# A retention layer and a gMLP block on one core: all five instruction queues in a new order, more warm-up matmuls, and a semaphore that one more kind of job may raise

## The chip, the core and the metric

The kernel runs on one core of a Trainium2 chip. TensorE (PE) multiplies matrices; its weight loads are listed apart as PEld. VectorE (DVE), ScalarE (ACT) and GpSimd (POOL) do elementwise work. SyncE (SP) issues the DMAs, which 16 DMA engines carry out. Each engine works through its own queue strictly in the order in which the program was written, and engines wait for each other by semaphores. TensorE writes its results to PSUM, which is split into banks; ACT and DVE read them from there. The metric is the device time of one execution in microseconds (us).

## The reference, cut to what matters

```python
B, H, S, D = 8, 8, 576, 64
scores = scale * np.matmul(q, k.transpose(0, 1, 3, 2))
ret = scores * Dmat[None]            # Dmat[h, s, t] = gamma[h] ** (s - t) for s >= t, else 0
x = np.matmul(ret, v)                # heads side by side: (8, 576, 512)
h = gelu(x @ w_in)                   # 512 -> 1024, tanh form
u, v = h[..., :512], h[..., 512:]
v_n = (v - mean) / np.sqrt(var + 1e-6) * g_ln
v_s = np.einsum('ts,bsd->btd', w_sg, v_n) + b_sg[None, :, None]
out = x + (u * v_s) @ w_out
```

## The kernel before, in words

Because `Dmat` is a product of powers, the attention is computed in blocks with a running state. The eight sequences go in four pairs `p`; a pair has nine row tiles of 128 rows, in five blocks (line 158). Block 0 of a pair holds one tile (64 rows of each sequence); blocks 1 to 4 hold two tiles each. So there are 20 blocks `b` (0, 5, 10 and 15 are the small ones) and 36 tiles `i`.

For each block, SP loads q, k and v (`a_load`, lines 338 to 351: 512 KB each, 1024 KB for the q of two blocks together, 2 x 128 KB in a small block). `a_prep` (line 364) casts them to bf16 and multiplies q and v by powers of gamma, on POOL except in block 0, where DVE takes q and ACT takes k. TensorE transposes q and k (`a_T`, line 431) and DVE brings them out of PSUM (`a_Tev`, line 450). TensorE forms the scores (`a_S`, line 492, one or two halves `g` a block), and DVE masks them (`a_Sev`, lines 505 and 508). `a_Z` (line 532) forms the state terms k'v, which DVE adds to the running state (`a_Zsum`) and ACT rounds (`a_Zev`). `a_O` (line 568) adds up the attention output of a block: 16 or 32 small matmuls for the block itself and 8 for the state terms whose rows of the array go with the bank they write. The other 8, the swapped state terms, come in a job of their own, `a_O2` (line 614): another part of the array adds into a place that `a_O` has just written, so they may start only when `a_O`'s matmuls have ended. ACT brings the output out of PSUM as bf16 (`a_Oev`, line 636), and this is the input `x` of the block that follows.

For each tile, `m_V` (line 647) makes the v half (4 matmuls with 512 columns), ACT applies gelu (line 654), DVE takes mean and variance (lines 662, 663), POOL makes the factors (`m_rs`, lines 667 to 670) and ACT normalises (`m_norm`, lines 679 and 682). `m_U` (line 697) makes the u half, with gelu on ACT (line 707). When five tiles of a sequence are ready, eight jobs `m_W` (line 715) multiply by `w_sg`, and DVE multiplies with u (`m_Wg`, line 725). `m_O` (line 745) multiplies by `w_out`; x is added, and `m_store` writes the tile out.

How `a_O2` waits is decided when the program is written (lines 396 to 416 and 614 to 619). `a_O` of any block but a pair's first sets `pend[b] = None`. The next job on TensorE that calls `mark` lets one of its first matmuls raise the semaphore `swap`; since matmuls end in order, that tells that `a_O` has ended, and `a_O2` waits for the count. If no such job comes between, `a_O2` begins with `nc.tensor.drain()`: TensorE starts nothing until all its matmuls have ended. Before the change, jobs of `a_T`, `a_S`, `a_Z`, `m_V`, `m_U`, `m_W` and `m_O` call `mark`; `a_O` does not, nor does `build_wT`. A matmul that raises `swap` does not carry the usual semaphore of its job, so the reader of the job's result is tied to its last matmul (`fence`, `unfence`).

Weights: the halves of `w_in` come as 1024 KB each (`win_load`, line 256: half 1 is for V, half 0 for U), and DVE and ACT cast one part each (lines 273 and 275). `w_sg` is loaded in three parts, cast (line 304), and transposed by `build_wT`; `w_out` follows.

The order of all queues is a list, `ORDER` (line 20): job numbers in the order in which the program is written, so each engine's own queue is the list cut down to that engine. An entry `f1`, `f2` or `f4` is a filler (lines 234 to 240): a matmul of zeros in f32 of 128, 256 or 512 columns, which the profile shows as two instructions, on a PSUM bank that nobody reads. Fillers stand among TensorE's jobs before the first tiles. PSUM has two buffers `pp` (transposes, scores, attention outputs) and four buffers `d` (all else, fillers too); of the load buffers `ld` there are eight. `Planner.run` (line 91) gives each new tile the buffer whose last user stands earliest in the list, so a new order also changes who waits for whose buffer.

Of the kernel before, what the change touches and what calls it, by code (L numbers as in the profile page):

```python
# [14 lines left out]
Act = mybir.ActivationFunctionType  # L15
# [2 lines left out]
PR = dict(PB0=10000.0, O=4000.0, PB=9900.0, S=2000.0, S2=400.0, Z=1901.0, V=6000.0, V2=900.0, U=1260.0, W=4000.0, WS=19000.0, slack=60.0, pen=500.0)  # L18

ORDER = (  # L20
# [33 lines left out]
)  # L54


# [56 lines left out]
def kernel(  # L113
# [12 lines left out]
    nc = tc.nc  # L126
# [199 lines left out]
    cur = {}  # L326
# [71 lines left out]
    def mark(ins, what):  # L398
        waiting = [b for b, on in pend.items() if on is None]
        if waiting:  # L400
            cur["swap"] = cur.get("swap", 0) + 1
            ins.then_inc(swap, 1)
            tc.no_tile_sem_insts.add(ins.ins.name)
            fenced[what] = f"swap{cur['swap']}"
            tc.add_to_no_dep_group(fenced[what], ins.ins)
            for b in waiting:
                pend[b] = cur["swap"]

    def fence(ins, what):
        if what in fenced:  # L410
            tc.declare_fence(ins.ins, group=fenced[what])
# [156 lines left out]
    def a_O(b):  # L568
        ns, zs = RB[b % NBK][0], st.pop((b, "zs"))
        cs = 64 * ns  # L570
        ot = psP.tile([128, 2, 512], F32, name="pp", tag=bank("pp"))
        st[b, "ot"] = ot
        begun = set()

        def mm(bank, kk, hh, lhsT, rhs):
            c = kk % 2
            j = 2 * hh + kk // 2
            nc.tensor.matmul(ot[64 * c:64 * c + 64, bank, j * cs:(j + 1) * cs], lhsT, rhs,  # L578
                             start=(bank, c) not in begun, stop=True, skip_group_check=True)
            begun.add((bank, c))  # L580

        def ap(hh, bank):
            zb = zs[bank]
# [22 lines left out]
        for n in range(max(len(P[0]), len(P[1]))):  # L606
            for l in P:
                if n < len(l):
                    l[n]()
        if b % NBK:  # L610
            st[b, "O2"] = (ap(0, 1), ap(1, 0))
            pend[b] = None
# [13 lines left out]
    def a_Oev(b, c, eng="ACT"):  # L626
        p, n = divmod(b, NBK)
        ns, m, _ = RB[n]
        cs = 64 * ns
        if n == 0 and c == 0:  # L630
            xTs[p] = new("xT", [128, NT, KK, 128], BF)
        tile_, col = (m + c, 0) if ns == 2 else (m, cs * c)
        s_ = ns if joint(b) else 4
        dst = xTs[p][:, tile_, :, col:col + cs].rearrange("p j (i s) -> p j i s", s=s_)
        src = st[b, "ot"][:, c, :KK * cs].rearrange("p (j s i) -> p j i s", j=KK, s=s_)
        nc.scalar.activation(dst, src, Act.Copy)  # L636


    vgs, mvs, vns = {}, {}, {}
# [498 lines left out]
```

## Time and profile before

| what | value |
| --- | --- |
| time of a run, median of three | 207.34 us (207.1 to 207.71) |
| the profiled execution's own time | 208.13 us |
| its span in the profile | 206.4 us |
| mean granted TensorE clock in it | 0.965 |
| TensorE matmuls busy | 190.6 us, 92% of the span |
| weight loads, DVE, ACT, POOL busy | 129.5, 144.6, 117.3, 118.4 us |

How to read it: the span runs from the first to the last instruction of the profiled execution, and 1.7 us of its own time lie outside. An engine's busy time is the sum of its instructions without overlaps. The two lines of digits over the span that matter here are PE, the busy share of each slice of 5.16 us in tenths, and PEclk, the clock that TensorE was granted, in tenths of full speed. In lists, a group has its line of the kernel, the engine, the operation, the tile that it writes `<-` what it reads, the shapes and the count. In the chain of waits, each piece has its start, its length, and the engine with the line that ended last; `SPq` is SP issuing a DMA.

### The profile page before, as it was taken

How to read it: one execution, taken by the hardware profiler on the slowest of the kernel's cores; microseconds unless marked ns; L12 is line 12 of the kernel's file. 1: busy time of each engine (PE TensorE's matmuls, PEld its weight loads, DVE VectorE, ACT ScalarE, POOL GpSimd, SP SyncE). 2: the span in 40 equal slices, each digit the busy share in tenths (PEclk: the TensorE clock that was granted, in tenths of full speed). 3: DMA queues.
4: the chain of work that ended last, by engine and by line, in shares of the span. 5: the costliest groups of instructions: out<-in, count | busy, mean ns of one | idle time of the engine just before them, and what ended most of it. 6: DMA issues, size and time to landing. Idle time of an engine off the chain costs nothing.

```text
span 206.4 us, 7490 instructions
## 1 busy us (share of the span) xinstructions
PE 190.6 (92%) x3183; PEld 129.5 (63%) x3212; DVE 144.6 (70%) x281; ACT 117.3 (57%) x210; POOL 118.4 (57%) x167
## 2 busy tenths in 40 slices
PE   5946899999999999999999999999999999999991
PEld 3525647667757767567675675676576585566760
DVE  4268559886795768836982788477977788476672
ACT  5045739796787745777547636756535765335300
POOL 8594299969839999516993575960594260022000
PEclk9995579999999999999999999999999999999999
DMA  6999999999999848969999999999979983939455
GB/s 154 258 340 330 388 350 242 267 357 375 300 263 342 273 123 121 260 146 352 274 235 196 303 242 258 238 258 292 328 177 218 169 244 107 204 91 215 139 144 205
DMA packets 93908, 50.45 MB, mean 244 GB/s; under 512 B 45034, under 2 KB 87282, under 8 KB 93874
## 3 DMA queue, kind: packets, MB, share of 16 engines
q1 hardware_dynamic: 93856, 49.96, 93.0%
q8 instruction: 25, 0.41, 0.8%
q14 instruction: 9, 0.07, 0.1%
q10 hardware_dynamic: 18, 0.00, 0.0%
HBM read 32.79 MB, written 9.44 MB: 205 GB/s over the span
## 4 chain that ended last, share of the span: by engine, by line
PE 84%; DMA 10%; issue 2%; ACT 1%; SPq 1%; DVE 0%
PE wp L715 20%; PE hu L697 16%; PE hv L647 15%; PE op L745 15%; PE pp L578 7%; DMA uT<-in_moe_w_in_dram 5%; PE pp L492 4%; PE pp L431 3%; PE zp L532 2%; DMA ld<-in_moe_w_sg_dram 2%; DMA ld<-in_k_dram 2%; PE op L740 1%; PE wtp L839 1%; SPq L351 1%; ACT xT L636 1%
## 5 line engine op out<-in xcount | busy, mean ns | idle before, releaser
L505 DVE TENSOR_TENSOR ret<-pp,msk 128x1024 bf16<-128x1024 f32 x32 | 38.6, 1216 | 8.0 <-PE pp L492 7.9
L715 PE MATMUL wp<-wT,vn 128*128 128x288 bf16 x256 | 40.8, 286 | 0.0
L654 ACT ACTIVATE vg<-hv 128x512 f32<-128x512 f32 x36 | 21.2, 595 | 28.0 <-PE hv L647 17.7
L647 PE MATMUL hv<-w_in,xT 128*128 128x512 bf16 x128 | 35.8, 388 | 1.4 <-issue 0.3
L394 POOL TENSOR_TENSOR vb<-ld,gpow 128x1024 bf16<-128x1024 f32 (+1 forms) x20 | 34.4, 1730 | 4.3 <-DVE uT L725 4.0
L725 DVE TENSOR_TENSOR uT<-wp,uT 128x288 bf16<-128x288 f32 x64 | 27.6, 450 | 12.8 <-PE wp L715 10.4
L697 PE MATMUL hu<-xT,w_in 128*128 128x256 bf16 (+1 forms) x320 | 35.7, 262 | 0.1
L745 PE MATMUL op<-w_out,uT 128*128 128x512 bf16 (+1 forms) x135 | 33.9, 373 | 0.6
L667 POOL TENSOR_SCALAR mv<-mv 128x2 f32<-128x2 f32 (+1 forms) x20 | 4.5, 224 | 50.8 <-DVE mv L663 50.1
L697 PEld LDWEIGHTS <-w_in 128*128 128x128 bf16 x320 | 27.9, 98 | 5.5 <-issue 0.3
L715 PEld LDWEIGHTS <-vn 128*128 128x128 bf16 x256 | 25.1, 98 | 8.0
L394 POOL TENSOR_TENSOR qb<-ldq,gpow 128x1024 bf16<-128x1024 f32 x14 | 26.5, 1901 | 5.3 <-DMA ldq<-in_q_dram 5.3
L662 DVE BATCH_NORM_STATS2 bst<-vg 128x6 f32<-128x512 f32 x36 | 24.6, 682 | 6.9 <-ACT vg L654 6.7
L636 ACT ACTIVATE xT<-pp 128x512 bf16<-128x512 f32 (+1 forms) x40 | 20.9, 549 | 14.2 <-PE pp L578 14.2
L682 ACT ACTIVATE vn<-vg,mv 128x512 bf16<-128x512 f32 x32 | 25.5, 808 | 4.0 <-POOL mv L670 3.8
L707 ACT ACTIVATE uT<-hu 128x512 bf16<-128x512 f32 x36 | 21.0, 593 | 10.8 <-PE hu L697 10.8
L765 DVE TENSOR_TENSOR ob<-op,xr 128x512 f32<-128x512 f32 (+1 forms) x28 | 18.3, 667 | 8.7 <-PE op L745 5.2
L647 PEld LDWEIGHTS <-xT 128*128 128x128 bf16 x144 | 13.8, 100 | 13.6 <-issue 1.4
L745 PEld LDWEIGHTS <-uT 128*128 128x128 bf16 x148 | 13.8, 98 | 11.9
L715 PE MATMUL wp<-wT,vmid 128*128 128x288 bf16 x64 | 18.4, 288 | 0.0
L668 POOL TENSOR_TENSOR mv<-mv,mhalf 128x2 f32<-128x2 f32 (+1 forms) x20 | 13.7, 685 | 1.7
L384 POOL CAST kb<-ld 128x1024 bf16<-128x1024 f32 x14 | 14.3, 1038 | 0.0
(104 smaller groups left out, 234.2 us busy)
## 6 DMA issues: line engine op xcount, KB each, us to landing
ld<-in_k_dram SPq DMA_DIRECT2D x16, 512.0 KB, 8.1
ld<-in_v_dram SPq DMA_DIRECT2D x16, 512.0 KB, 6.3
out_dram<-ob SPq DMA_DIRECT2D x31, 256.0 KB, 3.6
ldq<-in_q_dram SPq DMA_DIRECT2D x7, 1024.0 KB, 8.7
out_dram<-ob SPq DMA_DIRECT2D x10, 128.0 KB, 3.5
xT<-in_moe_w_sg_dram SPq DMA_DIRECT2D x2, 576.0 KB, 8.3
ld<-in_k_dram SPq DMA_DIRECT2D x8, 128.0 KB, 4.0
ld<-in_v_dram SPq DMA_DIRECT2D x8, 128.0 KB, 3.6
```

What stands on the lines that cost most here:

```text
L394: ve.tensor_tensor(dst, src, g.unsqueeze(len(src.shape) - 1).to_broadcast(list(src.shape)), op=Alu.mult)
L505: ins = nc.vector.tensor_tensor(ret[:].rearrange("p r (k t) -> p (r k) t", k=2), sc[:].rearrange("p r (k t) -> p (r k) t", k=2), (msk2 if ...
L636: nc.scalar.activation(dst, src, Act.Copy)
L647: ins = nc.tensor.matmul(hv[:], xTs[p][:, m, kk, :], w_in[:, kk, F2:], start=(kk == 0), stop=(kk == KK - 1))
L654: unfence(nc.scalar.activation(vgs[i][:], cur.pop(("hv", i))[:], Act.Gelu_apprx_tanh), ("V", i))
L662: nc.vector.bn_stats(bst[:], vgs[i][:])
L682: nc.scalar.activation(vn[:], vg[:], Act.Identity, scale=mv[:, s, 2:3], bias=mv[:, s, 3:4])
L697: ins = nc.tensor.matmul(hu[:, n, :], w_in[:, kk, 128 * c:128 * c + 128], xTs[p][:, m:m + w, kk, :], start=(kk == 0), stop=(kk == KK - 1), ...
L707: unfence(nc.scalar.activation(uTs[p][:, c0:c1, u_at(m):u_at(m) + 128 * w], cur.pop(("hu", i, half))[:], Act.Gelu_apprx_tanh), ("U", i, half))
L715: ins = nc.tensor.matmul(ps[:], vns[NT * p + (4 * e + j if j else 0)][e][:, 128 * c:128 * c + 128], wT1[:, half * HS:half * HS + HS] if e ...
L725: ins = nc.vector.tensor_tensor(uTs[p][:, c, col:col + HS], cur.pop(("wp", b, c, half))[:], uTs[p][:, c, col:col + HS], op=Alu.mult)
L745: ins = nc.tensor.matmul(op[:], uTs[p][:, c, u_at(m):u_at(m) + 128], w_out[:, c, cs], start=(p >= XP and c == 0), stop=(c == KK - 1), skip ...
```

## The change

Two things change. First, `ORDER` is replaced as a whole. It holds the same 902 jobs, with 22 fillers (four f1, eight f2, ten f4: 60 units of 128 columns) in place of 14 (six f1, six f2, two f4: 26 units). The heads of the two lists:

```diff
-    '72 7 1 2 6 0 17 f2 f2 f2 75 22 f1 76 95 f2 73 101 102 97 f2 f1 79 f4 77 f4 f2 96 8 3 12 78 98 104 80 260 f1 '
-    '263 261 99 103 105 190 191 f1 100 264 4 81 13 9 262 192 188 189 275 276 277 5 90 193 f1 265 11 f1 10 23 15 280 '
+    '73 f4 f2 f4 f4 6 f4 75 7 8 2 101 74 103 97 f2 102 1 0 17 f1 12 14 13 76 72 f4 f1 f2 79 f2 f2 77 f1 95 78 f4 96 '
+    'f4 80 260 261 98 104 99 105 262 275 f4 3 264 106 107 276 100 9 81 190 191 277 f2 f2 192 f4 22 193 f4 4 5 f2 '
...
```

Read engine by engine, the parts that the prediction speaks of become:

| queue | before | after |
| --- | --- | --- |
| SP, first loads | 1k 0k 0v 1q 0q, w_sg's last part, 1v, w_in half 1, 2q 2k, w_in half 0, 3q, w_sg, 2v, w_sg, 3k | 1q 1k 1v 0v 0k 0q, w_sg's last part, 2q 2v 2k, w_in half 1, w_in half 0, w_sg, 3q, w_sg, 3k |
| POOL, first | zeros, 1q 1k 0v 1v 2q 2k | zeros, 1q, zeros, 1v 0v 1k 2q 2k 2v |
| PE, before the first m_U | fillers, T0 T1 Z0, f1, S1, f1, S1 S0 Z1, build_wT, f1, O0, f1, O1 O2 of 1, T2, V0 V1 V2, S2 S2 | fillers, Z0 T0 T1 Z1, f4, S1, f2 f2, S1, f4 f4 f2, S0, O1 O0, O2 of 1, Z2, f1, T2, V0 |
| DVE around S0 | mask S1, cast w_in half 1, mask S0 | mask S1 twice, cast w_in half 1, mask S0 |
| ACT around the first outputs | cast w_in half 1, cast w_in half 0, Oev 0 0 1 1, gelu V0 | cast w_in half 1, Oev 0 0 1, cast w_in half 0, Oev 1, gelu V0 |

(1k is the load or preparation of block 1's k; S1 is a half of block 1's scores, and so on. `Oev` brings a bank of an attention output out of PSUM.) Later on, the same jobs are shifted against each other on every queue.

Second, `a_O` calls `mark` with its first matmul, and its two readers are tied to its last matmul:

```diff
@@ a_O
-            nc.tensor.matmul(ot[64 * c:64 * c + 64, bank, j * cs:(j + 1) * cs], lhsT, rhs,
-                             start=(bank, c) not in begun, stop=True, skip_group_check=True)
+            ins = nc.tensor.matmul(ot[64 * c:64 * c + 64, bank, j * cs:(j + 1) * cs], lhsT, rhs,
+                                   start=(bank, c) not in begun, stop=True, skip_group_check=True)
+            if not begun:
+                mark(ins, ("O", b))
             begun.add((bank, c))
+            cur["last"] = ins
...
+        fence(cur["last"], ("O", b))
         if b % NBK:
             st[b, "O2"] = (ap(0, 1), ap(1, 0))
             pend[b] = None
@@ a_Oev
-        nc.scalar.activation(dst, src, Act.Copy)
+        read = cur["evicted", b] = cur.get(("evicted", b), 0) + 1
+        unfence(nc.scalar.activation(dst, src, Act.Copy), ("O", b), read == 2)
```

Where the lists put jobs around a swapped step: before, `a_O2` follows its `a_O` with nothing that marks between for block 1, for block 2 (`build_wT` stands between), for block 3, and in three places where two outputs and then their two swapped steps come in a row (blocks 11 and 12, 13 and 14, 18 and 19). After, nothing that marks stands between for blocks 2 and 3 alone; another block's `a_O` is the first job that marks for blocks 1, 9, 12 and 13.

62 rows, old and new, of the table ORDER are left out of this document.

## The prediction, as it was put on record

> **What bounds the kernel now.** I read the page first, for which engine is full, then stretches of the span, then the chain of waits where TensorE is not full.
>
> ```profile
> span 206.4 us, 7490 instructions
> PE 190.6 (92%) x3183; PEld 129.5 (63%) x3212; DVE 144.6 (70%) x281; ACT 117.3 (57%) x210; POOL 118.4 (57%) x167
> ```
>
> ```profile
> 10.32:15.48 5.16, 2.20 (x68) 1.41 (x66) 3.37 (x7) 2.33 (x5) 5.16 (x4) 0.91 1.05 340
> 14.60:28.25 13.65, 9.89 (x195) 7.05 (x196) 9.17 (x12) 7.41 (x14) 6.21 (x5) 0.50 1.07 361
> 26.40:31.00 4.60, 4.58 (x55) 2.36 (x55) 2.70 (x5) 1.77 (x4) 4.60 (x3) 0.80 1.08 348
> 31.00:46.00 15.00, 14.42 (x351) 10.28 (x352) 13.70 (x24) 13.37 (x25) 12.69 (x18) 1.00 1.01 287
> 56.00:196.00 140.00, 137.96 (x2284) 93.59 (x2293) 101.78 (x189) 82.93 (x149) 76.28 (x102) 1.00 0.94 225
> ```
>
> The columns are start and end, length, busy time of PE, PEld, DVE, ACT and POOL, granted clock, DMA share, GB/s. There are three stages. Up to 31 us TensorE waits and, from 14.60 to 28.25, has half its clock. From 31 to 46 it is nearly full, but so are DVE (13.70 of 15) and ACT (13.37). From 56 on TensorE alone is full: 2.04 us idle in 140. The last tile leaves in the new list as it does now. Since the work is the same, a reorder gains at the front or hardly at all. What holds the front is in the chain:
>
> ```profile
> 12.24 11.13 DMA uT<-in_moe_w_in_dram
> 23.39 1.06 ACT w_in L275
> 24.45 0.55 ACT xT L636 x2
> 25.05 1.04 PE pp L431 x32
> 26.42 3.45 PE hv L647 x11
> ```
>
> Half 0 of w_in lands at 23.39; ACT casts it first, only then brings out the attention output (24.45), and only then come a transpose and m_V, at half clock.
>
> **The front after the change.** First the weights, by the bytes queued ahead of them.
>
> ```profile
> 7.98 1.28 SPq L266 DMA_DIRECT2D xT<-in_moe_w_in_dram  x1
> ```
>
> ```profile
> xT<-in_moe_w_in_dram SPq DMA_DIRECT2D x1, 1024.0 KB, 8.4
> ```
>
> Half 1 was issued at 7.98 and took 8.4, so it landed at 16.4, with 3472 KB queued up to and with it (sizes from the code). In the new list that sum is 5008 KB: blocks 0, 1 and 2 whole, w_sg's last part, the half itself. The 1.57 MB more, at 340 to 361 GB/s, are 4.4 to 4.6 us. I take 20.9. Half 0 follows at once: 1.05 MB at 361 is 2.9 us, so 23.8, about where it is now.
>
> ```profile
> 18.64 1.21 DVE L273 TENSOR_REDUCE w_in<-xT 128x1024 bf16<-128x1024 f32 x1
> 19.77 0.68 DVE L508 TENSOR_TENSOR ret<-pp,msk 128x512 bf16<-128x512 f32 x1
> ```
>
> ```profile
> 24.36 1.61 ACT L636 ACTIVATE xT<-pp 128x256 bf16<-128x256 f32 x4
> ```
>
> ```profile
> 29.80 0.64 PE L492 MATMUL pp<-qT 64*64 64x128 bf16 x32
> 30.37 1.94 PE L697 MATMUL hu<-xT,w_in 128*128 128x128 bf16 x24
> 32.24 0.64 PE L431 MATMUL pp<-ident,qb 64*128 64x64 bf16 x32
> 32.81 0.25 PE L842 MATMUL wtp<-ident,wnat 128*64 128x128 bf16 x2
> 32.99 0.40 PE L839 MATMUL wtp<-ident,wnat 128*128 128x128 bf16 x4
> ```
>
> ```profile
> 162.93 1.73 PE hv L647 x8
> ```
>
> In DVE's new queue the cast of half 1 stands ahead of the masking of S0, so the first output hangs on that landing: 20.9 + 1.21 cast + 0.68 mask + 0.3 (an estimate: 16 small matmuls) for O0 + 2 x 0.40 to bring it out = 23.9. Then T2 (0.57, from 32.24 to 32.81) and V0 (0.87, half of the 1.73): 25.3. On the other side ACT does one more output (0.40) and the cast of half 0 (1.06): 25.4. So the first m_U starts near 25.5, against 30.37. Queued behind the waiting O0 are the swapped step of block 1, Z2, a filler and T2; they fall into the time in which ACT works.
>
> ```profile
> 44.57 1.04 PE L647 MATMUL hv<-w_in,xT 128*128 128x512 bf16 x3 [0.23 <-ACT xT L636]
> ```
>
> Not all of the 4.9 us is won. The place to compare is V6, a tile of block 3, at 44.57: what follows it on TensorE is the same set of jobs in both lists but for one half of S4. From the first m_U to V6 it is 14.2 us now. In the new list this stretch also holds V1 and V2 (1.73), three halves of scores (0.57 for two in the row at 29.80, so 0.86) and a build_wT (about 0.5), and no longer Z2 (about 0.4), and I take out 0.9 for waits that it has now: 14.2 + 1.73 + 0.86 + 0.5 - 0.4 - 0.9 = 16. V6 could start at 41.5.
>
> Two things stand against that. **The clock.** The row at 10.32 has PE busy for 2.20 of 5.16, and at 14.60 the clock fell to half until 28.25, four steps of 3.41. In the new list fillers cover PE until S0 (about 20); then it has O1, O0, a swapped step, Z2 and a filler, about 1.5 us in 3.4, before T2 at 23.9. Steps on the same grid end at 21.4, 24.8 and 28.3, so I expect half clock from 24.8 to 28.3, which costs half of that, 1.7 us.
>
> ```profile
> 12.38 0.41 PE L431 MATMUL pp<-ident,qb 64*128 64x64 bf16 x16 [1.75 <-ACT qb L382]
> ```
>
> [...]
>
> **ACT and DVE.** Between 26.4 and 46 DVE idles 1.90 + 1.30 = 3.2 us and ACT 2.83 + 1.63 = 4.5. Most of their work up to V6 is the same, so hardly more than 3.2 us can be won by then. V6 itself waited for ACT. ACT has 1.77 + 13.37 in those two rows and 1.61 before them, less about 1.3 that lies behind V6, and now one cast (1.06) more: 16.5, so from 23.1 it ends at 39.6 with no idle at all, and it has to wait for POOL and TensorE in between. I put V6 at 42.7: between 41.5 with neither and 43.2 with the clock's loss whole. That is 1.9 us earlier. From V6 to 56 I take back 0.6 (an estimate; bounds 0 and 1.2), because m_W needs five normalised tiles and ACT comes straight from a full stretch.
>
> **Fillers.**
>
> ```profile
> 9.08 1.56 PE L239 MATMUL scr<-ob 128*128 128x512 f32 x4
> ```
>
> Four instructions are f4 and f2, six units: 0.26 a unit. 34 units more are 8.8 us of TensorE. I cost them at nothing: what covers them is the landing of half 1. All but one of the 60 stand ahead of T2, 15.3 us between 1.5 and 20.9, and the real jobs there are some 3 us. If that cover were gone they would cost up to 8.8.
>
> **The semaphore.**
>
> ```profile
> 66.24 0.31 PE L578 MATMUL pp<-qT,zb 64*64 64x128 bf16 x8
> 66.38 0.62 PE L578 MATMUL pp<-ret,vb 64*64 64x128 bf16 x32
> 66.82 0.39 PE L492 MATMUL pp<-qT,kT 64*64 64x128 bf16 x16
> 67.12 0.31 PE L578 MATMUL pp<-qT,zb 64*64 64x128 bf16 x8
> 67.36 0.30 PE L715 MATMUL wp<-wT,vmid 128*128 128x288 bf16 x1
> ```
>
> ```profile
> 107.81 0.28 PE L578 MATMUL pp<-qT,zb 64*64 64x128 bf16 x8
> 107.92 0.62 PE L578 MATMUL pp<-ret,vb 64*64 64x128 bf16 x32
> 108.66 0.73 PE L578 MATMUL pp<-qT,zb 64*64 64x128 bf16 x16
> 109.32 0.68 PE L697 MATMUL hu<-xT,w_in 128*128 128x128 bf16 x9
> ```
>
> Where a job that marks stands between, a_O takes 66.82 - 66.24 = 0.58 from start to start and the swapped step 67.36 - 67.12 = 0.24. With two drains a_O takes 108.66 - 107.81 = 0.85, and both swapped steps 0.66 in place of 0.48: 0.27 + 0.18 = 0.45 a pair. The three pairs (blocks 11 and 12, 13 and 14, 18 and 19) lose their drains: 1.35. The new wait stands ahead of the swapped step with all of TensorE's queue behind it, but the matmul that raises it is 15 or more matmuls back, so I take 0 (bounds 0 and a drain's 0.27, four times). Single drains at blocks 2 and 3 stay; block 1's is inside the front.
>
> [...]
>
> **The full stretch.** After 56 us the order of m_V, m_W and m_U against ACT and DVE is new throughout, and each tight place costs some tenths where TensorE now idles 2.04 us, drains included. I take 0.6 worse (an estimate; bounds 0.5 better and 1.8 worse).
>
> The sum: 1.9 - 0.6 + 1.35 - 0.6 = 2.05 us off. The profiled execution (208.13, span 206.4) would take 206.1 with a span of 204.4; the median of the runs, 0.79 below the profiled time, goes from 207.34 to 205.3. A measurement tells 0.3%, 0.62 us, from no change: 206.72 to 207.96 counts as the same.
>
> **Rivals.**
>
> *The weights come too late, and it is slower.* Place: SP's queue. Ahead of w_in now stand the loads 2v and 2k, which take the buffers of 1q and 1v and so wait for POOL.
>
> ```profile
> 9.69 1.90 POOL L394 TENSOR_TENSOR qb<-ld,gpow 128x1024 bf16<-128x1024 f32 x1 [2.21 <-DMA ld<-in_q_dram]
> ```
>
> I have 1q, now the first load, there when POOL ends its zeros at 9.69 - 2.21 = 7.5; then 1v ends near 11.7 and half 1 is issued near 12.2. If 1q comes at 9.69 as in this row, half 1 is issued at 14.5 and lands 8.4 later at 22.9, half 0, with its 11.13 from 15.5, at 26.6. The first m_U starts near 28 and V6 at 44, with the clock's loss at 45.7; the later losses stay, at their bounds 1.2 and 1.8, and the drains give 1.35: about 0.9 slower in the middle, 208.2. It decides when half 0 lands after 26.5. Chance 0.15.
>
> *The catch-up costs nothing.* The clock stays whole and ACT keeps pace: V6 at 41.5, 3.1 earlier, 0.3 lost behind: 3.1 + 1.35 - 0.3 = 4.15 off, 203.2. Against it stands the row of 31 to 46. Chance 0.15.
>
> *The change does not do what it says*: the swapped steps wait for their states and not for the drain, or new waits eat the 1.35. Then 2.05 - 1.35 = 0.7 off, 206.6, up to no change. For it: V6 shows a wait for ACT that outlasts the drain ahead of it. Against: no releaser stands in the row at 108.66. Chance 0.25.
>
> **How the numbers follow.** My forecast, 204.4 to 206.4, has 0.45, the rivals 0.15, 0.15 and 0.25. The range, 203.3 to 207.9, leaves out about half of the fast rival and most of the slow one. Faster: 0.45 + 0.15 + 0.10 of the third = 0.70. Same: 0.15 of the third and 0.02 of the slow one = 0.17. Slower: 0.13.
>
> **What would show it.** In the new profile: half 1 cast by DVE near 21 and half 0 by ACT near 24; the first hu near 25.5; half clock for at most one or two steps; V6 between 41.5 and 43.5; pairs of outputs without the 0.27; TensorE idle 2 to 3 us from 56 on. I am wrong if V6 is not before 44, or if the stretch after 56 loses more in waits than it wins from drains.

## The result, and the profile after

| what | before | after |
| --- | --- | --- |
| time of a run, median of 20 | 207.04 us (205.90 to 209.27) | 206.46 us (203.62 to 211.99) |
| the profiled execution's own time | 208.13 us | 205.94 us |
| its span | 206.4 us | 204.2 us |
| mean granted clock in it | 0.965 | 0.995 |

The ratio of after to before is 0.9934, with a 95% interval of 0.9905 to 0.9962: 0.7% faster. Measured a second time, beside the experiments, it was 0.9967 (0.9937 to 0.9996), 0.3% faster. Medians and ranges hold every execution, but ratios leave out those over 1.5% longer than the shortest of their kernel (nine of the changed kernel's 20 here, one of the 20 before), and the profiles of two experiments, the one without the mark and the one with one-unit fillers, are of this kind, so the times of their stages are not compared. The medians of the table differ by 0.58 us, 0.3%. So the gain is 0.3 to 0.7%, and the smaller figure has more behind it.

The page of the changed kernel, span, engines and clock:

```profile
span 204.2 us, 7548 instructions
PE 195.8 (96%) x3228; PEld 128.9 (63%) x3228; DVE 146.6 (72%) x281; ACT 117.2 (57%) x210; POOL 118.2 (58%) x167
PEclk9999999999999999999999999999999999999997
```

TensorE is busy for 5.2 us more in a span that is 2.2 us shorter: its fillers take 18.0 us in place of 10.1, and all else takes 2.7 less. The granted clock falls only in the last slice, to 0.50 at 202.0, behind the last matmul (199.87). The same stretches of the span as ahead of the prediction (start and end, length, busy time of PE, PEld, DVE, ACT and POOL, granted clock, DMA share, GB/s):

```profile
10.32:15.48 5.16, 5.16 (x62) 2.94 (x62) 4.66 (x6) 0.35 (x1) 3.49 (x3) 1.00 1.04 307
14.60:28.25 13.65, 12.80 (x305) 8.39 (x304) 11.21 (x17) 9.73 (x19) 5.67 (x6) 1.00 0.92 324
31.00:46.00 15.00, 14.00 (x340) 9.44 (x338) 13.54 (x22) 13.08 (x25) 13.24 (x16) 1.00 1.00 274
56.00:196.00 140.00, 139.41 (x2291) 93.25 (x2284) 102.05 (x190) 81.91 (x146) 75.91 (x101) 1.00 0.95 234
```

From 14.60 to 28.25 the clock is 1.00 where it was 0.50. From 56 on TensorE idles 140 - 139.41 = 0.59 us, where it idled 2.04. Single instructions of the changed kernel, on DVE, ACT and PE (start, length, what it is, and in brackets the idle time ahead of it with what ended it):

```profile
20.41 1.21 DVE L273 TENSOR_REDUCE w_in<-xT 128x1024 bf16<-128x1024 f32 x1
23.86 1.21 DVE L273 TENSOR_REDUCE w_in<-uT 128x1024 bf16<-128x1024 f32 x1
```

```profile
24.08 1.07 ACT L275 ACTIVATE w_in<-uT 128x1024 bf16<-128x1024 f32 x1
27.07 1.25 ACT L304 ACTIVATE wnat<-xT 128x576 bf16<-128x576 f32 x2 [0.94 <-DMA xT<-in_moe_w_sg_dram]
```

```profile
25.28 1.93 PE L702 MATMUL hu<-xT,w_in 128*128 128x128 bf16 x24
28.38 0.25 PE L847 MATMUL wtp<-ident,wnat 128*64 128x128 bf16 x2 [0.66 <-ACT wnat L304]
43.60 1.04 PE L652 MATMUL hv<-w_in,xT 128*128 128x512 bf16 x4 [0.23 <-ACT xT L641]
```

The first m_U (line 702 now) starts at 25.28, 5.1 us earlier than before. V6, the point after which TensorE has the same work in both lists but for one half of S4, starts at 43.60, only 0.97 earlier than its 44.57. So four fifths of the head start are gone again within 18 us. The last matmul ends at 199.87 against 202.25. From V6 to there it is 156.27 against 157.68, another 1.41 less. With 0.22 more behind the last matmul, -0.97 - 1.41 + 0.22 = -2.16: the 2.2 us of the span.

The chain of waits of the changed kernel begins like this (some of its longest pieces up to 27 us; `scr` is what a filler writes):

```profile
1.50 7.07 PE scr L239 x10
8.73 2.37 PE scr L239 x10
17.81 1.06 PE scr L239 x4
19.27 1.23 DVE ret L505
20.50 1.14 DVE w_in L273
21.65 5.39 DMA xT<-in_moe_w_sg_dram
```

Up to 19 us it goes through TensorE, mostly through fillers, then over DVE's mask of S1 to its cast of half 1; no load of w_in is in it.

Three questions are open: what the fillers did, where the head start went, and what the 1.41 are.

### The profile page after: what moved, and what is told of

Read it like the earlier page. It is cut to its first block, busy times and chain, and to the rows that moved or that the text cites. A ratio compares the mean times of both kernels' runs of the same rounds, so it can differ in the third digit from the quotient of the medians.

```text
span 204.2 us, 7548 instructions
## 1 busy us (share of the span) xinstructions
PE 195.8 (96%) x3228; PEld 128.9 (63%) x3228; DVE 146.6 (72%) x281; ACT 117.2 (57%) x210; POOL 118.2 (58%) x167
## 4 chain that ended last, share of the span: by engine, by line
PE 84%; DMA 6%; ACT 4%; DVE 3%; issue 0%; POOL 0%; ACTq 0%
PE wp L720 18%; PE op L750 15%; PE hv L652 14%; PE hu L702 14%; PE scr L239 7%; PE pp L578 5%; PE pp L492 5%; DMA kT<-kb 3%; DMA xT<-in_moe_w_sg_dram 3%; PE zp L532 2%; PE pp L431 2%; PE op L745 1%; ACT xT L641 1%; ACT vmid L684 1%; PE wtp L844 1%; ACT wnat L304 1%
## 5 line engine op out<-in xcount | busy, mean ns | idle before, releaser
L652 PE MATMUL hv<-w_in,xT 128*128 128x512 bf16 x144 | 36.9, 380 | 0.4 <-ACT xT L641 0.2
L702 PE MATMUL hu<-xT,w_in 128*128 128x256 bf16 (+1 forms) x320 | 36.5, 262 | 0.1
L750 PE MATMUL op<-w_out,uT 128*128 128x512 bf16 (+1 forms) x148 | 35.9, 374 | 0.0
L659 ACT ACTIVATE vg<-hv 128x512 f32<-128x512 f32 x36 | 21.4, 596 | 22.6 <-PE hv L652 19.6
L702 PEld LDWEIGHTS <-w_in 128*128 128x128 bf16 x320 | 28.4, 98 | 6.4 <-DVE uT L730 0.3
L652 PEld LDWEIGHTS <-xT 128*128 128x128 bf16 x144 | 12.9, 98 | 13.0 <-ACT xT L641 1.8
L239 PE MATMUL scr<-ob 128*128 128x512 f32 (+2 forms) x44 | 18.0, 550 | 1.5 <-DVE ob L197 1.5
```

The lines of the kernel that those rows point to most:

```text
L239: nc.tensor.matmul(scr[:, :128 * n], warm[:, :128], warm[:, :128 * n], start=True, stop=True, skip_group_check=True)
L652: ins = nc.tensor.matmul(hv[:], xTs[p][:, m, kk, :], w_in[:, kk, F2:], start=(kk == 0), stop=(kk == KK - 1))
L659: unfence(nc.scalar.activation(vgs[i][:], cur.pop(("hv", i))[:], Act.Gelu_apprx_tanh), ("V", i))
L702: ins = nc.tensor.matmul(hu[:, n, :], w_in[:, kk, 128 * c:128 * c + 128], xTs[p][:, m:m + w, kk, :], start=(kk == 0), stop=(kk == KK - 1), ...
L750: ins = nc.tensor.matmul(op[:], uTs[p][:, c, u_at(m):u_at(m) + 128], w_out[:, c, cs], start=(p >= XP and c == 0), stop=(c == KK - 1), skip ...
```

## The experiments

Stages of the profiled executions, in us:

| kernel | first m_U | V6 | end of the last matmul | V6 to there |
| --- | --- | --- | --- | --- |
| before | 30.37 | 44.57 | 202.25 | 157.68 |
| after | 25.28 | 43.60 | 199.87 | 156.27 |
| after, measured again | 25.20 | 43.63 | 200.67 | 157.04 |
| old order, with the mark | 31.57 | 45.77 | 202.38 | 156.61 |
| after, drains put back | 25.61 | 44.50 | 202.58 | 158.08 |
| after, no fillers | 25.72 | 44.23 | 202.03 | 157.80 |
| old order, longer fillers | 28.60 | 42.80 | 200.74 | 157.94 |
| after, build_wT later | 25.21 | 43.62 | 199.37 | 155.75 |
| after, 3q earlier | 25.51 | 43.98 | 200.63 | 156.65 |
| after, 3q earlier and more | 25.56 | 44.64 | 202.33 | 157.69 |
| after, 2v later | 25.14 | 43.77 | 200.86 | 157.09 |
| after, 2v and build_wT later | 25.14 | 44.03 | 200.22 | 156.19 |

The changed kernel stands there twice: V6 agrees within 0.03 us, and the stretch behind it differs by 0.77. So V6 can be read to some tenths in one profile, and the rest of the kernel hardly to a whole microsecond, unless a difference can be put down to single instructions. Here it can, in the main: of the 0.77, TensorE loses 0.28 ahead of an m_W at 49.4 and 0.65 ahead of one at 132.7 (133.7 when measured again), and gets 0.2 back later. The kernel before has one profile only, so its 157.68 may be off by as much.

### The two parts apart

**The new order without the mark.** `a_O` and `a_Oev` are those of before.

```diff
-            if not begun:
-                mark(ins, ("O", b))
...
-        fence(cur["last"], ("O", b))
```

> The new order with a_O as it was before, so that it raises no semaphore. Three swapped steps then begin with a drain that they do not have in the changed kernel: those of blocks 1, 9 and 13 (blocks 11 and 12 find Z13 between, 14 finds an m_W). Theory (a drain costs 0.27 after an output, and most of the drains were taken away by the order, not by the semaphore): 0.27 at 9 and 13 each, nothing at 1, where TensorE waits for the first attention output anyway: about 0.5 us slower than the changed kernel, so 0.9 us faster than the kernel before. Rival (the semaphore carries the gain from the swapped steps): all of 1.35 us is lost, and it is level with the kernel before.

Median 207.89 us (205.12 to 209.53), ratio to before 1.0000 (0.9958 to 1.0043). That is 0.3 to 0.7% over the two measurements of the changed kernel, but the intervals overlap. It is level with before, as the rival had it; the theory's 0.9 us under before would be a ratio of 0.9957, just outside the interval. So the time speaks for the rival, and weakly; the count of the drains below does not.

**The old order with the mark.** Only the second part of the change.

```diff
+            if not begun:
+                mark(ins, ("O", b))
...
+        fence(cur["last"], ("O", b))
```

> The old order with the semaphore in a_O: the other half alone. In each of the three pairs (11 and 12, 13 and 14, 18 and 19) the second output raises the semaphore for the first, so that the first swapped step waits for it, and the second still begins with a drain. Theory: the 0.27 after the outputs goes, the drain between the two swapped steps stays and may grow from 0.18 to 0.25: 0.5 to 0.8 us faster than before. Rival (what is won is eaten by waits behind, since DVE and ACT have to follow): within 0.3 us of before.

Median 206.83 us, ratio 0.9966 (0.9929 to 1.0003): 0.7 us, in the expected direction, with an interval that just reaches no change. From V6 to the last matmul it is 1.07 less than before, not much more than two profiles of one kernel differ by.

What each part does to the drains can be counted in the lists: a swapped step drains when no job that marks stands between it and its `a_O`. Ten drain before (blocks 1, 2, 3, 9, 11, 12, 13, 14, 18, 19), five with the new order alone (1, 2, 3, 9, 13), seven with the mark alone (1, 2, 3, 9, 12, 13, 19), two with both (2, 3). So most of the drains go because the order puts other jobs between, and the mark removes three more. How the gain in time divides between the two is not settled.

### The price of a drain

**The changed kernel with drains put back** at the seven places behind V6 at which the kernel before drains.

```diff
-        if on is None:
+        if on is None or b in (9, 11, 12, 13, 14, 18, 19):
             nc.tensor.drain()
```

> The changed kernel, in which the swapped steps of blocks 9, 11, 12, 13, 14, 18 and 19, which drain in the kernel before, drain again in place of their wait. Theory: the 1.4 us won between V6 and the last matmul (157.68 before, 156.27 after) are the drains: 157.7 again, and 1.4 us slower than the changed kernel (0.2 a drain). Rival: the drains are hidden, the swapped steps would wait for their states anyway, and the 1.4 us come from the order of the tiles: 156.3, level with the changed kernel.

Measured: median 207.56 us, ratio 0.9977 (0.9940 to 1.0014), beside 0.9967 for the changed kernel on the same chip. The time cannot tell the two apart. The trace can. TensorE around the swapped steps of blocks 12 and 11, first in the changed kernel (measured again), then with the drains:

```profile
108.81 0.42 PE L532 MATMUL zp<-vb,kb 64*64 64x64 bf16 x32
109.06 0.43 PE L578 MATMUL pp<-qT,zb 64*64 64x128 bf16 x16
109.42 0.30 PE L720 MATMUL wp<-wT,vmid 128*128 128x288 bf16 x1
```

```profile
109.64 0.42 PE L532 MATMUL zp<-vb,kb 64*64 64x64 bf16 x32
110.28 0.70 PE L578 MATMUL pp<-qT,zb 64*64 64x128 bf16 x16 [0.21 <-issue]
110.91 0.30 PE L720 MATMUL wp<-wT,vmid 128*128 128x288 bf16 x1
```

From the start of Z13 to the start of the m_W behind the two steps it is 0.61 without and 1.27 with two drains: 0.66. In the same way, from the job ahead to the job behind: block 9 0.32, block 13 0.32, block 14 0.15, block 18 0.18, block 19 0.17. Together 0.66 + 0.32 + 0.32 + 0.15 + 0.18 + 0.17 = 1.80 us for seven. The rival, that the steps wait for their states anyway, falls: each place got longer when the drain came back. But not all of it reaches the end. From the outputs of blocks 9 and 8 (83.3) to the last matmul, TensorE takes 1.39 longer than in the changed kernel measured again, because waits at 129.7 and 133.7 became 0.22 and 0.19 shorter. (From V6 to the last matmul the difference is 1.04 against that profile and 1.81 against the first; that 1.81 lies so near to 1.80 is chance.)

### What the fillers do

**The changed kernel without fillers**, then **with each filler cut to one unit** (22 units in place of 60):

```diff
-    '73 f4 f2 f4 f4 6 f4 75 7 8 2 101 ...
+    '73 6 75 7 8 2 101 ...
```

> The changed kernel without any filler; everything else in the same order (some PSUM buffers change hands). Theory (the fillers are there for the clock; what holds the front is the landing of w_in): TensorE has under half of its time to do up to 23 us, the clock falls to half and is back only two or three steps of 3.41 after the first m_V; the first m_V stays near 24.4 or comes 0.3 earlier, and the m_V and m_U up to about 28 to 31 us take twice as long: 2 to 4 us lost there, of which some is hidden behind DVE and ACT: 1 to 3 us slower than the changed kernel. Rival (the fillers hold the queue and do nothing for the rest): 0 to 0.5 us faster than the changed kernel, since S0 comes earlier.

> The changed kernel with its 22 fillers at the same places, each cut to one unit: 22 units in place of 60 (the kernel before has 26). Theory: what counts is that TensorE's clock has stopped rising and falling before the first m_V, and for that the units count, not the number of fillers; with 22 units the clock is half in part of 14 to 28 again, the first hu comes at 25.3 to 25.7 (the landing of half 0 holds it), V6 0.5 to 1 later, and the time is 1 to 3 us over the changed kernel, as without fillers. Rival (the prediction's: fillers cost and bring nothing): level with the changed kernel, or up to 0.5 faster, since S0 no longer stands behind fillers.

Without fillers: median 209.89 us, ratio 1.0093 (1.0056 to 1.0129), slower than before. With one-unit fillers: 209.12 us, ratio 1.0045 (1.0002 to 1.0088). Both lose the whole gain and more. With one-unit fillers the mean granted clock was 0.973 to 0.992 in all twelve executions, where the changed kernel's twelve beside other experiments had 0.996 to 1.000. Without fillers the trace has its first record of the full clock at 27.62, and up to there TensorE's matmuls take longer; its m_V and m_U at the front:

```profile
24.04 1.89 PE L652 MATMUL hv<-w_in,xT 128*128 128x512 bf16 x4
25.72 2.84 PE L702 MATMUL hu<-xT,w_in 128*128 128x128 bf16 x24
```

The same 24 matmuls took 1.93 in the changed kernel, and the four of V0 1.04.

The fillers are not free either. S0 of the changed kernel stands behind three of them (f4 f4 f2), DVE's mask waits for it, and everything up to the first m_U follows. First the changed kernel, then the same point and ACT's cast of half 0 without fillers:

```profile
19.68 1.88 PE L239 MATMUL scr<-ob 128*128 128x512 f32 x5
21.50 0.32 PE L492 MATMUL pp<-qT 64*64 64x64 bf16 x16
21.94 0.69 DVE L508 TENSOR_TENSOR ret<-pp,msk 128x512 bf16<-128x512 f32 x1 [0.32 <-PE pp L492]
```

```profile
19.03 0.43 PE L492 MATMUL pp<-qT 64*64 64x64 bf16 x16 [0.97 <-DVE ret L505]
21.15 0.68 DVE L508 TENSOR_TENSOR ret<-pp,msk 128x512 bf16<-128x512 f32 x1
23.38 1.07 ACT L275 ACTIVATE w_in<-uT 128x1024 bf16<-128x1024 f32 x1
```

Without fillers the mask comes 0.79 earlier, the cast of half 0 0.70 (23.38 in place of 24.08) and V0 0.36, though the clock is not full there. So the fillers hold the front back by some tenths of a microsecond, and by the clock they bring more than that.

In the profile without fillers V6 is only 0.6 later; that execution was the shortest of its twelve, and what the others lose beyond it is not seen in it and stays open.

**The old order with longer fillers.** The kernel before, each of its 14 fillers at its place with four units: 56 in place of 26.

```diff
-    '72 7 1 2 6 0 17 f2 f2 f2 75 22 f1 76 ...
+    '72 7 1 2 6 0 17 f4 f4 f4 75 22 f4 76 ...
```

> The kernel before with its 14 fillers at their places, each lengthened to four units: 56 units in place of 26 (the changed kernel has 60). Theory: the longer fillers alone keep the clock whole from 14.60 to 28.25, at no cost, since they stand under waits for data; the first m_V (26.42, 3.45 for 11 matmuls) runs at full clock, hu starts 1 to 2 earlier than at 30.37, V6 0.5 to 1.5 earlier than 44.57, and the time is 0.5 to 1.5 less than the kernel before. Rival: the landing of half 0 and the outputs hold the front, and the clock falls in spite of them or costs nothing: level with the kernel before, or slower by up to 1 where fillers delay S and O.

Median 206.60 us (206.10 to 207.46), ratio 0.9975 (0.9950 to 1.0000). The stretches of the front:

```profile
10.32:15.48 5.16, 5.16 (x81) 2.32 (x79) 1.96 (x3) 1.69 (x3) 5.16 (x4) 1.00 1.05 344
14.60:28.25 13.65, 11.61 (x283) 6.32 (x286) 10.39 (x15) 8.18 (x15) 7.45 (x5) 1.00 1.07 350
```

and TensorE's instructions in it:

```profile
25.33 2.76 PE L648 MATMUL hv<-w_in,xT 128*128 128x512 bf16 x12
28.60 1.94 PE L698 MATMUL hu<-xT,w_in 128*128 128x128 bf16 x24
42.80 1.04 PE L648 MATMUL hv<-w_in,xT 128*128 128x512 bf16 x4 [0.23 <-ACT xT L637]
```

The clock stays at 1.00, the twelve m_V matmuls take 2.76 in place of 3.45 (of which the earlier row has recorded eleven), and V6 starts at 42.80: 1.77 earlier than before, and 0.80 earlier than in the changed kernel, whose first m_U starts 3.3 earlier. (In the old order V6 also moves with the place of the half clock: in the profile with the mark that is 16.95 to 30.60, and V6 is at 45.77.) So in these profiles the clock alone gives more at V6 than the whole change does, and the new order of the front gives some of it back. In the time of the whole kernel the two cannot be told apart (0.9975 and 0.9967).

### Where the head start goes

From the first m_U to V6 the stretch holds, by PE's busy time, 13.67 us of work in 14.20 before and 16.66 in 18.32 after:

```profile
30.37:44.57 14.20, 13.67 (x358) 10.01 (x352) 12.81 (x21) 12.59 (x23) 12.38 (x16) 1.00 1.00 278
```

```profile
25.28:43.60 18.32, 16.66 (x399) 11.40 (x397) 14.98 (x23) 14.53 (x27) 14.11 (x16) 1.00 1.01 295
```

Of the 5.09 us, 0.97 is left at V6. 2.99 went to jobs that did not stand in this stretch before (V1, V2, two halves of S2 and a build_wT from ahead of it, a half of S4 from behind it, less Z2), and 1.13 to waits: 1.66 in place of 0.53. Five experiments took one of these waits away each, or made something come earlier.

**build_wT 4 and 1 behind V1**, so that the wait of 0.66 for w_sg at 28.38 holds up nothing that is ready:

```diff
- ... 271 292 19 90 293 16 84 85 194 24 196 31 195 91 197 284 113 ...
+ ... 271 292 19 293 16 194 24 196 31 195 197 284 90 84 85 91 113 ...
```

> In the changed kernel TensorE waits 0.66 us at build_wT of part 1, from 27.7 to 28.4, for ACT's cast of w_sg, whose load was issued only at 21.65. Here the two jobs build_wT 4 and 1, and their two copies on DVE, are put behind V1; nothing else is moved. Theory A (that wait is what kept V6 at 43.6 in place of 42.7): V6 comes 0.6 to 0.9 us earlier and so does the end. Theory B (DVE and ACT are full up to 46 us, so a hole of TensorE's that is closed early opens again later): V1 and U1 come 0.8 earlier, V6 moves by less than 0.3, and the time stays within 0.3 us of the changed kernel.

Ratio 1.0013 (0.9977 to 1.0048). On TensorE:

```profile
27.64 1.04 PE L653 MATMUL hv<-w_in,xT 128*128 128x512 bf16 x4
30.34 1.03 PE L703 MATMUL hu<-xT,w_in 128*128 128x256 bf16 x8 [0.65 <-DVE wT L853]
31.21 1.03 PE L653 MATMUL hv<-w_in,xT 128*128 128x512 bf16 x4
```

V1 starts 1.82 earlier, and V2 where it was (31.20): a wait of 0.65 for DVE, which brings the transposed w_sg out of PSUM, has taken the place of the 0.66 for ACT.

**The load 3q ahead of w_sg**, since POOL's work on block 3 waited 1.13 us for it; then the same with POOL taking 3q ahead of the factors of tile 0, and the work on w_sg moved back:

```diff
- ... 188 189 278 15 23 108 ...
+ ... 188 189 278 23 15 108 ...
```

> The changed kernel with one load moved: the load 3q goes ahead of the w_sg part that waits for the cast of half 1 of w_in. Theory: in the new order V6 is held by POOL's work on block 3, whose first instruction waits for 3q (29.79, 1.13 us of wait; V6 at 43.60, 13.8 us behind). 3q then lands about 1.7 us earlier, POOL starts on it at 28.7 (m_rs of tile 0 stands ahead of it), V6 starts near 42.5 and the kernel takes about 1 us less than the changed one. Rival: the full stretch of ACT and DVE from 31 to 46 holds V6; then POOL starts earlier but V6 stays at 43.6 or moves later by what ACT waits longer for w_sg (up to 2 us).

> As the run with 3q ahead of w_sg, and what would wait for w_sg is moved back: ACT's casts of it behind the gelu of V1, build_wT 4 and 1 behind V2; POOL takes 3q ahead of m_rs of tile 0. Theory (3q through POOL holds V6): POOL starts on 3q at 27.0 to 28.1, V6 at 41 to 42, the whole 1.5 to 2.5 us under the changed kernel. Rival (ACT and DVE hold V6): V6 stays within 0.5 of 43.6 and the time is level with the changed kernel.

Ratios 1.0022 (0.9988 to 1.0057) and 0.9981 (0.9947 to 1.0015). POOL started on 3q at 28.85 and at 27.08 in place of 29.79, as expected; V6 came at 43.98 and 44.64, later and not earlier. The theory that block 3 holds V6 by way of POOL is gone. The rival named for both, ACT and DVE, fits, but so does TensorE's own queue: from V2 to V6 it is 12.40 or 12.41 us in the changed kernel (twice) and in the runs without fillers, with build_wT later, with 3q ahead of w_sg, with 2v later (both) and with drains put back, wherever V2 falls, but not for the second of these two, where the build_wT that were moved lie in that stretch (14.07) and which therefore says little of 3q.

> The changed kernel itself, as it is, beside the three others on one chip. Theory (3q through POOL holds V6): its V6 stands 13.8 us behind POOL's start on 3q again, wherever that start falls; a later landing of 3q moves V6 and the end by as much. Ratio to the kernel before 0.993, as in the result. Rival: V6 at 43.6 whatever 3q does.

This run gave the second ratio above, 0.9967. Its POOL starts on 3q at 29.82 and its V6 is at 43.63, which both theories allow.

**The load 2v (512 KB) behind both halves of w_in**, and Z2 behind the first m_U; then, with that, build_wT 4 and 1 behind V1:

```diff
- ... 1 0 17 f1 12 14 13 76 ... 100 9 81 ... 281 297 266 f1 267 263 298 ... 271 ...
+ ... 1 0 17 f1 12 13 76 ... 100 9 14 81 ... 281 266 f1 267 263 ... 271 297 298 ...
```

> The changed kernel with the load 2v (512 KB) moved behind both halves of w_in, and with it Z2 behind the first m_U. Theory: the landing of half 0 sets the first m_U, and V6 stands 18.3 to 18.5 us behind that, 16.7 of them TensorE's own work; half 0 lands 1.5 us earlier (512 KB at 340 GB/s), the first hu starts near 23.8, V6 near 42.3, the kernel takes 1.4 less than the changed one. Rival: V6 is held by what comes by other ways (w_sg, 3q through POOL): V6 stays at 43.6, the wait ahead of build_wT 4 grows from 0.66 to about 2, and the time is level.

> As the run with 2v behind w_in, and build_wT 4 and 1 behind V1, so that a later w_sg holds no TensorE work that is ready. Theory (TensorE's own work behind the first m_U sets V6): V6 at 42 or a little before, 1.5 less than the changed kernel. Rival (other data hold V6): V6 at 43.6, level with the changed kernel.

Ratios 0.9974 (0.9937 to 1.0011) and 1.0006 (0.9969 to 1.0043). The casts of half 0 with 2v later, by DVE and by ACT:

```profile
23.14 1.21 DVE L274 TENSOR_REDUCE w_in<-uT 128x1024 bf16<-128x1024 f32 x1
```

```profile
24.01 1.07 ACT L276 ACTIVATE w_in<-uT 128x1024 bf16<-128x1024 f32 x1
```

Half 0, issued at 12.72 in place of 14.05, has landed by 21.8 (9.1 after its issue). DVE casts it 0.72 earlier, since the sum that follows Z2 no longer stands ahead, but ACT still does so at 24.01, because three outputs stand ahead of it in its queue and those hang on S0, which stays at 21.42. The first m_U moves by 0.14, and V6 is 0.17 later. So in the changed kernel the landing of half 0 no longer sets the first m_U; the chain from S0 over DVE's mask, O0 and ACT does, and S0 comes when the fillers ahead of it have ended. With build_wT later too, V1 starts at 28.05, and the next m_U waits again:

```profile
30.76 0.49 PE L703 MATMUL hu<-xT,w_in 128*128 128x256 bf16 x3 [0.66 <-DVE wT L853]
```

None of the five moved V6 ahead of 43.6. Where the rows show it (a wait for DVE in place of one for ACT, ACT's outputs in place of the landing), each wait that was removed had another one close behind it.

## Why the prediction was right, and where it was not

The direction and the range were right. The time of the runs was forecast at 205.3 and came out at 206.46, just outside the "204.4 to 206.4" of the forecast itself: 0.6 of the 2.05 us by the medians, 1.4 by the ratio of 0.9934. The profiled execution came within 0.2 us of its 206.1, but that agreement comes from errors that cancel, and from which execution was profiled (206.47 when measured again).

**The front up to the first m_U** was right in its times: DVE's cast near 21 (20.41), ACT's near 24 (24.08), hu at 25.5 (25.28). Its chain was not. "The first output hangs on that landing" put half 1 at 20.9. It was issued at 12.27 and took 7.2, so it had landed at 19.5, and DVE's cast shows no wait for it: it follows the two masks of S1, which end TensorE's chain of fillers and scores. Without fillers, too, it follows the masks, at 20.02. That the two chains end within 0.5 us of each other is luck.

**The clock** was wrong. "I expect half clock from 24.8 to 28.3" did not happen: PE's longest gaps from 1.50 to V6 are 0.31, 0.35 and 0.66 us, and the clock held. The step also took the places at which the clock may change from the profile before (21.4, 24.8, 28.3), and they shift between executions: it fell at 14.60 in one profile of the old order and at 16.95 in the other. The length of the steps, 3.41 us, is an estimate from the profile before, where the recorded stretches of one clock last 10.24 (full, to 14.60), 13.65 (half, to 28.25) and 177.49 us (full, to 205.75), close to 3, 4 and 52 times 3.413. "I cost them at nothing" was nearly right for the fillers, some tenths of a microsecond, but the reason was not: "what covers them is the landing of half 1", and the chain of waits goes through them. What they are worth has no term in the sum: the chain to the first m_U is simply added up at full clock, where the kernel before ran at half for 13.65 us, 14.60 to 28.25. The old order with longer fillers shows that worth by itself: 1.77 us at V6.

**V6** is the term that was mis-sized: 1.9 earlier was forecast, 0.97 was measured, later even than the bound "43.2 with the clock's loss whole", with no clock loss at all. One part of its sum failed. The moved jobs were put at 1.73 + 0.86 + 0.5 - 0.4 = 2.69 and measured 2.99, nearly right. But the step took out 0.9 for waits that the stretch had then, where it had only 0.53, and the new stretch has 1.13 more of them. The prediction looked for one engine that would hold V6 (ACT, with its 16.5 us); the runs show several, a few tenths apart. Which of them would be last once all the others were moved is not settled.

**Drains**: 1.35 forecast, 1.80 where they stand when all seven are put back, 1.39 of it at the end. A pair was put at 0.45; measured are 0.66 for blocks 11 and 12, 0.32 + 0.15 for 13 and 14, 0.18 + 0.17 for 18 and 19, and 0.32 for block 9, which was not counted. Two things were wrong. The text counted six drains behind V6, and the lists have a seventh, block 9's. And it took them for the work of the mark alone, where the new order by itself removes five of the seven.

**The losses behind V6**, 0.6 up to 56 us and 0.6 in the full stretch, are not settled. From V6 to the last matmul the changed kernel gains 1.41 on the kernel before in the first profile and 0.64 in the second. Set against the 1.80 of the drains, it loses 0.4 in the one and 1.2, just what was forecast, in the other. The sign that was named for it, TensorE idle for 2 to 3 us from 56 on, did not come: it idles 0.59 and 1.03 there, where it idled 2.04. One place where it waits in both, 0.45 and 0.37:

```profile
138.70 0.42 PE L492 MATMUL pp<-qT,kT 64*64 64x128 bf16 x16 [0.45 <-DMA kT<-kb]
```

So 1.9 + 1.35 - 1.2 = 2.05 became 0.97 + 1.41 = 2.38 in the first profile, 2.16 with what lies behind the last matmul; by the second it is 0.94 + 0.64 = 1.58.

**The rivals.** The weights did not come late: half 1 landed 1.4 before the time that the forecast gave it. Of the third rival one half fell with the drains put back: the swapped steps do wait for the drain. The other half, "new waits eat the 1.35", is not refuted: its 206.6 is the figure nearest to the medians of 206.46 and 206.55, and by the second profile most of the 1.80 is gone again. The fast case is right in one point, since the clock stayed whole; its V6 at 41.5 did not come, because "ACT keeps pace" was not the only condition: TensorE's own 16.66 us from 25.28 already end at 41.94 with no wait at all.

By the medians the gain is smaller than by the first two profiles. The profiled execution of before is longer than most of its kind (208.13 against a median of 207.04 in 20), the first one of the changed kernel shorter (205.94 against 206.46). The ratio of 0.9934 makes 1.4 us, the second, 0.9967, 0.7.

The longer fillers in the old order and the removal of drains add up on paper: V6 at 42.80 and 156.27 behind it would end the last matmul at 199.1 (an estimate from two profiles), 0.8 before the changed kernel. That combination was not run.

## What to carry to other kernels

Price warm-up work by what the clock does over the whole front, not only by the time that it takes: the same fillers cut to one unit turned a gain of some tenths of a per cent (0.9934 and 0.9967) into a loss of half a per cent (1.0045). When jobs move, do not stop at the first event that comes earlier; take a later point with the same work behind it in both orders, and count the work and the waits up to there. An event that comes at the forecast time does not show that the forecast's chain led to it: look at what it waited for. And count what a code change does in the new list and in the old one, since the order alone may already do most of it.

## What the runs showed of the hardware

**The clock fell after gaps of under 2 us, and in one of 3.24.** Before, it fell at 14.60 after gaps of 1.75, 0.30 and 0.37 us; in the old order with the mark it fell at 16.95, in a gap of 1.91 behind gaps of 0.71 and 0.37; in the old order with longer fillers it held through a single gap of 1.27 (at 16.72). With one-unit fillers it fell at 14.15, in the gap of 3.24 that this row shows:

```profile
14.83 0.43 PE L533 MATMUL zp<-vb,qb 64*64 64x64 bf16 x16 [3.24 <-DVE row4b L815]
```

In the kernel before, no gap ahead of the fall is over 1.75 us, and the last three are waits for ACT and POOL. How long a gap has to be for the clock to fall these runs do not show: it fell with 1.75, 1.91 and 3.24 us and held with 1.27.

**Much work with short gaps did not raise it.** Without fillers TensorE worked for 10.71 of the 13.65 us from 14.60 to 28.25, with gaps of 0.44 to 0.97 in the part up to 21.88, and the first full clock is recorded at 27.62. The page of that kernel prints full clock in its first slices too, and its mean clock is 0.998: neither shows that the matmuls take longer at first, which has to be read from the durations (2.84 us at 25.72 for 24 matmuls that take 1.93). The changed kernel starts so too, though its row prints full clock there: its first ten filler instructions, 18 units, take 7.07 us, 0.39 a unit, where a unit took 0.26 in the row of the prediction.

**Loads that land just in time.** From 46 us on POOL waits for loads in several places of the changed kernel, where it waited 1.0 us in all before:

```profile
86.41 1.04 POOL L394 TENSOR_TENSOR qb<-ld,gpow 128x512 bf16<-128x512 f32 x1 [4.21 <-DMA ld<-in_q_dram]
122.95 3.77 POOL L394 TENSOR_TENSOR qb<-ldq,gpow 128x1024 bf16<-128x1024 f32 x2 [0.96 <-DMA ldq<-in_q_dram]
142.59 1.90 POOL L394 TENSOR_TENSOR vb<-ld,gpow 128x1024 bf16<-128x1024 f32 x1 [4.98 <-DMA ld<-in_v_dram]
```

The runs of the new order also spread more widely: 205.2 to 208.7 us for the changed kernel measured again, 206.1 to 207.5 for the old order with longer fillers, twelve runs each. At one place the two profiles of the changed kernel show how a load that lands later reaches TensorE. These are POOL's preparation of a block's k, and the m_W at which the second profile loses 0.65, in the first profile and then measured again:

```profile
128.44 1.04 POOL L384 CAST kb<-ld 128x1024 bf16<-128x1024 f32 x1 [1.17 <-DMA ld<-in_k_dram]
132.65 0.29 PE L720 MATMUL wp<-wT,vmid 128*128 128x288 bf16 x1
```

```profile
129.53 1.04 POOL L384 CAST kb<-ld 128x1024 bf16<-128x1024 f32 x1 [1.31 <-DMA ld<-in_k_dram]
133.67 0.28 PE L720 MATMUL wp<-wT,vmid 128*128 128x288 bf16 x1 [0.48 <-ACT vg L659]
```

POOL waits longer for q (1.54 us in place of 0.96) and then for k, so the factors of a tile pair that follow on POOL are 1.1 late, where TensorE's work up to there is 0.4 late, and so are ACT's normalisation and the gelu behind it, for which TensorE then waits. Whether this makes the whole difference in spread is not shown.
